# The experts of ranks 2 to 7 of a second mixture, written out twice in the arms of a conditional

## The chip, the cores and the metric

The kernel runs on one core of one Trainium2 chip. It is one launch that computes a local attention and two mixtures of experts. The metric is the device time of that launch in microseconds (us). TensorE (PE) does the matmuls, PEld loads their weights, VectorE (DVE), ScalarE (ACT) and GpSimd (POOL) do the rest; SyncE (SP) and other engines issue the transfers. Each engine runs its own instructions in order, and waits for others by semaphores.

## The reference

Attention over 4 x 8 x 576 x 64 gives 2304 tokens of 512 numbers. They go through a first mixture (a token has one expert, and some tokens skip it), and the result `x` goes through a second, in which each token has two of eight experts:

```python
def _moe2_ref(x, w_gate, w_noise, noise, w1, w2):     # x: 2304 x 512, w1: 8 x 512 x 1024, w2: 8 x 1024 x 512
    logits = x @ w_gate
    noise_scale = np.log1p(np.exp(x @ w_noise))
    noisy_logits = logits + noise_scale * noise
    top2 = np.argpartition(-noisy_logits, 2, axis=1)[:, :2]
    ...
    for e in range(E):
        for k in range(2):
            mask = top2[:, k] == e
            ...
            h = np.maximum(x[mask] @ w1[e], 0.0)
            out[mask] += top2_w[mask, k, None] * (h @ w2[e])
```

How many tokens an expert has depends on the data. Worked out from the reference with the inputs as it draws them (seed 0), experts 0 to 7 of the second mixture have 578, 590, 570, 587, 592, 562, 548 and 581 tokens.

## The kernel before

The attention runs first, then the first mixture, then the second. In the second mixture an expert is an object `Second` with a fixed capacity: a number of token rows that its matmuls work on, whatever its count is. Experts 0 and 1 are always first, with a capacity of 640 (five blocks of 128 rows, `NB2 = 5`, `BLK2 = 128`). The others are ranked by their counts on the chip, and the expert of rank r gets `CAPS2[r]` rows. Tokens beyond a capacity would go to a loop at the end (`over2`, in a conditional on `n_over2`).

The steps of an expert are these:

- `gather` (POOL, L317 within): five indirect transfers fetch the rows of its blocks (`rows2`, five buffers).
- `prep(b)`: four transposes on PE (`pT`, L1632) turn a block; ACT and DVE split it into a high and a low part (`xh`, `xl`, L1634 and L1635).
- `up(f)`, f from 0 to 7: matmuls on PE (`pH`, L1647), three products for each of four slices of the inner dimension, and for each chunk of tokens; then ACT writes `hh` (L1651) and DVE writes `hl` (L1652). For ranks 2 to 7 the tokens are in two chunks, 256 wide and `cap - 256` wide. For experts 0 and 1 they are in the chunks `first` (384 wide) and `second` (256 wide), and all eight `up(f, first)` come before the eight `up(f, second)`.
- `down(b)`: 24 matmuls 512 wide for each block (`pY`, L1664), ACT scales the result (`yo`, L1666), and POOL adds it to the output by an indirect transfer (L322).

The weights of an expert come in four pieces for each matrix through three buffers `stg` (SP), and ACT and DVE cut each piece into a high and a low part (L1322 and L1323).

While expert 1's `up(f, first)` runs, DVE ranks the experts and sets their places, and `gates` spreads the gate weights: three casts and two subtractions on DVE (L331 to L335), then two large multiplications on POOL (L346, `w<-w,g`, 128x2160). The orders of PE, ACT, DVE and SP are those in which the code is written; POOL's order is set by a scheduler, which moves no instruction across a conditional.

The first mixture has a conditional of the kind that the change adds (`small1`, L1829): `larger` takes four short DVE steps (L482, L484, L493, L213) to write `beyond`, the number of experts whose count is above the smaller capacities. `n_beyond` then reads that number into a register of each engine (TENSOR_LOAD, L1699), and each engine compares and jumps.

Of the kernel before, what the change touches and what calls it, by code (L numbers as in the profile page):

```python
# [21 lines left out]
DM = H * D  # L22
E = 8
# [11 lines left out]
BLK1, NB1 = 112, 2  # L35
CAPS = (224, 200, 180, 164, 152, 144, 132, 120)
CAPS_S, JOIN = (204, 178, 166, 150, 140, 136), 6
CAPS2 = (640, 640, 632, 616, 604, 596, 584, 572)
DUMP1 = E * NB1 * BLK1
BLK2, NB2 = 128, 5  # L40
# [67 lines left out]
def moe_attention_kernel(ctx, tc, q, k, v, w_skip, w_gate, w1, w2, g2, n2, noise, u1, u2, out, dbg=None):  # L108
# [58 lines left out]
    def routing_constants():  # L167
        c.desc = iota([128, E], [[-1, E]], E, 0, "desc")
        c.e64 = iota([128, E], [[64, E]], 0, 0, "e64")
        c.rows = iota([128, 128], [[1, 128]], 0, 0, "rows")  # L170
        c.codes1 = iota([128, E * NB1], [[64, E], [1, NB1]], 1, 0, "codes1")
        c.codes2 = iota([128, E * NB2], [[64, E], [1, NB2]], 1, 0, "codes2")
        c.dump1 = iota([128, E * NB1], [[BLK1, E * NB1]], N + 1, 1, "dump1")
        c.dump2 = iota([128, E * NB2], [[0, E], [BLK2, NB2]], N + 1, 1, "dump2")
        tkf = rt.tile([128, NT, 2], F32, name="tkf")
        nc.gpsimd.iota(tkf[:, :, 0], pattern=[[128, NT]], base=0, channel_multiplier=0,
                       allow_small_or_imprecise_dtypes=True)
        nc.gpsimd.iota(tkf[:, :, 1], pattern=[[0, NT]], base=1, channel_multiplier=1,
                       allow_small_or_imprecise_dtypes=True)
        c.tk = rt.tile([128, NT, 2], BF, name="tk")  # L180
        nc.gpsimd.tensor_copy(c.tk, tkf)
        c.number = iota([128, E], [[1, E]], 0, 0, "number")
        c.caps, c.caps_s, c.caps2, c.fixed = (rt.tile([128, E], F32, name=n) for n in ("caps", "capss", "caps2", "fixed"))
        nc.gpsimd.memset(c.fixed, 0.0)
        for r in range(E):
            nc.gpsimd.memset(c.caps[:, r:r + 1], float(CAPS[r]))
            nc.gpsimd.memset(c.caps_s[:, r:r + 1], float((CAPS_S + CAPS[JOIN:])[r]))
            nc.gpsimd.memset(c.caps2[:, r:r + 1], float(CAPS2[r]))
        for r in range(AHEAD):
            nc.gpsimd.memset(c.fixed[:, r:r + 1], float(AHEAD - r))  # L190
        c.steps = iota([128, 40], [[1, 40]], 0, 0, "steps")
        t = iota([128, E, E], [[1, E], [-1, E]], 0, 0, "upto")
        nc.gpsimd.tensor_scalar(t, t, 0.0, None, op0=OP.is_ge)
        c.upto = t
        c.dump2_ahead = iota([128, AHEAD * (CH[0][1] // BLK2)], [[0, AHEAD], [BLK2, CH[0][1] // BLK2]], N + 1, 1, "dump2a")
# [19 lines left out]
    class Places:  # L215
# [140 lines left out]
    def run(steps, n=1000):  # L356
        for f in steps[:n]:
            f()
        del steps[:n]
# [942 lines left out]
    slots1[2:2] = [weight_slot(F32) for i in range(2)]  # L1302
    split = {}

    def split_weights(name, e, r=None):

        src = (u1 if name == 1 else u2)
        src = (src[e:e + 1] if r is None else src[ds(r, 1)]).rearrange("o (k p) f -> p (o k) f", p=128)
        c = src.shape[2]
        st = {}  # L1310

        def load():
            split[name, e] = (weight_slot(F32R), weight_slot(F32R))
            k = 1024 // c
            for i in range(4):
                st[i] = stg.tile([128, 1024], F32, name="stg")
                nc.sync.dma_start(st[i].rearrange("p (k f) -> p k f", f=c), src[:, i * k:(i + 1) * k, :])

        def cut(i):
            hi, lo = split[name, e]  # L1320
            c = slice(i * 1024, (i + 1) * 1024)
            nc.scalar.activation(hi[:, c], st[i], AF.Copy)  # L1322
            V.tensor_tensor(lo[:, c], st[i], hi[:, c].bitcast(F32), op=OP.subtract)  # L1323

        return load, [lambda i=i: cut(i) for i in range(4)]
# [276 lines left out]

    adds, h2 = [], []

    class Second:


        def __init__(self, e):
            self.e, self.cap, self.rows, self.x = e, CAPS2[e], [], {}
            self.chunks = CH if e < AHEAD else ((0, 256), (256, self.cap))  # L1610

        def block(self, b):
# [1 line left out]

        def gather(self, n, idx):
            for b in range(n):
                r = xp.tile([BLK2, DM + 16], F32, name="rows2", bufs=5)
                s = self.block(len(self.rows))
                m = s.stop - s.start
                gather(r[0:m], idx[0:m, b:b + 1])  # L1620
                self.rows.append(r)

        def prep(self, b):
            cols = self.block(b)
            n = cols.stop - cols.start
            a, z = next(ch for ch in self.chunks if ch[0] <= cols.start < ch[1])
            if a == cols.start:
                w = 256 if z - a == 256 else 384
                self.x[a, z] = [xp.tile([128, KD, w], F32R, name=f"{name}{int(w == 256)}") for name in ("xh", "xl")]
            p = bank("pT", [128, KD, n])  # L1630
            for k in range(KD):
                nc.tensor.transpose(p[:, k, :], self.rows[b][0:n, k * 128:(k + 1) * 128], ident[0:n, 0:n])  # L1632
            hi, lo = (t[:, :, cols.start - a:cols.stop - a] for t in self.x[a, z])
            nc.scalar.activation(hi, p, AF.Copy)  # L1634
            V.tensor_tensor(lo, p, hi.bitcast(F32), op=OP.subtract)  # L1635

        def up(self, f, chunks=None):
            chunks = chunks or self.chunks
            if f == 0 and chunks[0][0] == 0:
                self.h = [h2[0].tile([128, KF, CAP], F32R, name=n) for n in ("hh", "hl")]  # L1640
            wh, wl = (t.rearrange("p (k f) -> p k f", k=KD) for t in split[1, self.e])
            ps = [bank("pH", [128, b - a]) for a, b in chunks]
            fs = slice(f * 128, (f + 1) * 128)
            for k in range(KD):
                for i, (w, n) in enumerate(((wh, 0), (wh, 1), (wl, 0))):
                    for p, ch in zip(ps, chunks):
                        nc.tensor.matmul(p, w[:, k, fs], self.x[ch][n][:, k, 0:ch[1] - ch[0]], start=k == 0 and i == 0,  # L1647
                                         stop=k == KD - 1 and i == 2)
            for p, (a, b) in zip(ps, chunks):
                hi, lo = (t[:, f, a:b] for t in self.h)  # L1650
                nc.scalar.activation(hi, p, AF.Relu)  # L1651
                V.scalar_tensor_tensor(lo, p, 0.0, hi.bitcast(F32), op0=OP.max, op1=OP.subtract)  # L1652
# [256 lines left out]
    for f in range(KF):  # L1909
# [7 lines left out]
        elif f > 2:  # L1917
# [2 lines left out]
                run(cb, 1)  # L1920
            elif f < 7:
                x.prep(f - 5 + EARLY)
    run(gates)
    gidx2, sidx2 = whole.gidx, whole.sidx
    for f in range(KF):
        x.up(f, second)
        if f % 2:
            run(cb, 1)
    whole.gate_table()
    over2 = Overflow(lambda: whole.total, BLK2, NB2 - 1, 34, Carved(rt.tile([128, NT * BLK1 // 2], F32, name="room2", tag="lhs1")), rt,  # L1930
                     "ov2", cap_of)
    for e in range(1, E):
        x = ex2[e]
        ca = cb = []
        if e + 1 < E:
            r = nc.sync.value_load(order2[0:1, e + 1:e + 2], min_val=0, max_val=E - 1)
            la, ca = split_weights(1, e + 1, r)
            lb, cb = split_weights(2, e + 1, r)
            ex2[e + 1].gather(NB2, gidx2[:, (e + 1) * NB2:(e + 2) * NB2])
            la()  # L1940
        if e > 1:
            for f in range(KF):
                x.up(f)
                if f % 2:
                    run(ca, 1)
                elif e == 3:
                    run(over2.steps, 4)
        if e + 1 < E:
            lb()
        for b in range(NB2):  # L1950
            if e + 1 < E:
                if b == 0:
                    ex2[e + 1].prep(0)
                    ex2[e + 1].prep(1)
                elif b < 4:
                    ex2[e + 1].prep(b + 1)
            i = e * NB2 + b
            x.down(b, gt2[:, i:i + 1], sidx2[:, i:i + 1])
            for w in range(2 if e == 1 else 1):
                run(ca or cb, 1)  # L1960
    n_over2, ids2 = over2.number(), over2.ids
    with tc.If(n_over2 > 0):
        with tc.For_i(0, n_over2, 1) as i:
# [90 lines left out]
```

## Time and profile before

| what | value |
|---|---|
| median of 3 runs | 773.49 us (771.2 to 775.84) |
| the profiled execution | 766.73 us, of which its span is 765.0 us, with 1.73 us around it |
| PE busy in the span | 743.2 us (97%) |
| DVE, ACT, POOL busy | 348.6 us, 249.2 us, 254.4 us |
| second mixture: its first matmul to the span's end | 298.3 to 765.0 us |
| expert 1's `up(f, first)` and `up(f, second)` on PE | 360.06 to 391.5 us |
| experts of ranks 2 to 7, `up(0)` of the first to PE's last `down` | 423.98 to 758.45 us |

A busy time is what an engine worked, and not what it was waited for; the chain of waits tells which engine's work ended last at each point. [...]

### The profile page before, as it was taken

How to read it: one execution, taken by the hardware profiler on the slowest of the kernel's cores; microseconds unless marked ns; L12 is line 12 of the kernel's file. 1: busy time of each engine (PE TensorE's matmuls, PEld its weight loads, DVE VectorE, ACT ScalarE, POOL GpSimd, SP SyncE). 2: the span in 40 equal slices, each digit the busy share in tenths (PEclk: the TensorE clock that was granted, in tenths of full speed). 3: DMA queues.
4: the chain of work that ended last, by engine and by line, in shares of the span. 5: the costliest groups of instructions: out<-in, count | busy, mean ns of one | idle time of the engine just before them, and what ended most of it. 6: DMA issues, size and time to landing. Idle time of an engine off the chain costs nothing.

```text
span 765.0 us, 15204 instructions
## 1 busy us (share of the span) xinstructions
PE 743.2 (97%) x6217; PEld 655.7 (86%) x6217; DVE 348.6 (46%) x789; ACT 249.2 (33%) x492; POOL 254.4 (33%) x272
## 2 busy tenths in 40 slices
PE   6989899999999999999999999999999999999996
PEld 3567777999999999888998998998997997987984
DVE  6986887411112755659654343343342342342200
ACT  3445653111112243233335333233332333333211
POOL 8783422321223541133545015015025124003012
PEclk9899999999999999999999999999999999999999
DMA  8999559699998952234538436336336337233013
GB/s 280 302 283 292 150 169 331 163 387 386 350 331 283 354 166 65 95 61 122 158 97 223 132 112 162 83 111 162 81 122 155 83 120 171 75 97 43 9 21 42
DMA packets 60396, 130.59 MB, mean 171 GB/s; under 512 B 15674, under 2 KB 16496, under 8 KB 58784
## 3 DMA queue, kind: packets, MB, share of 16 engines
q1 hardware_dynamic: 30688, 55.85, 23.4%
q10 hardware_dynamic: 17248, 46.66, 17.2%
q0 software_dynamic: 12384, 27.03, 16.7%
q8 instruction: 51, 0.84, 0.4%
q14 instruction: 25, 0.20, 0.1%
HBM read 101.86 MB, written 23.73 MB: 164 GB/s over the span
## 4 chain that ended last, share of the span: by engine, by line
PE 84%; DMA 5%; DVE 3%; POOL 3%; issue 3%; ACT 1%; ACTq 0%; DVEq 0%; POOLq 0%; SPq 0%
PE pY L1664 28%; PE pH L1647 25%; PE pH L584 9%; PE pY L599 9%; PE pT L1632 2%; DMA v<-in_v 1%; DMA kT<-in_k 1%; DMA x_d<-x 1%; PE pB L1019 1%; PE pT L621 1%; PE pT L1036 1%; PE pB L895 1%; PE pT L563 1%; DMA up<-od 1%; DMA rows<-x_d,ix2g 1%
## 5 line engine op out<-in xcount | busy, mean ns | idle before, releaser
L1664 PE MATMUL pY<-w,hh 128*128 128x512 f32 (+6 forms) x640 | 202.4, 397 | 0.0
L1647 PE MATMUL pH<-xh,w 128*128 128x256 f32 (+7 forms) x1024 | 195.3, 302 | 0.1
L1647 PEld LDWEIGHTS pH<-xh,w 128*128 128x128 f32 x1024 | 162.3, 188 | 1.0 <-DVE hl L1652 0.3
L1664 PEld LDWEIGHTS pY<-w,hh 128*128 128x128 f32 (+6 forms) x640 | 115.1, 183 | 28.3
L1323 DVE TENSOR_TENSOR w<-stg,w 128x1024 fp32r<-128x1024 f32 x64 | 83.0, 1303 | 108.5 <-ACT w L1322 108.3
L1664 PE MATMUL pY<-w,hl 128*128 128x512 f32 (+6 forms) x320 | 126.1, 394 | 0.0
L1647 PE MATMUL pH<-xl,w 128*128 128x256 f32 (+7 forms) x512 | 123.0, 301 | 0.0
L1652 DVE SCALAR_TENSOR_TENSOR hl<-pH,hh 128x256 fp32r<-128x256 f32 (+7 forms) x128 | 56.9, 473 | 127.9 <-ACT hh L1651 127.7
L322 POOL DMA_INDIRECT out<-yo,ix2w x35 | 67.7, 1934 | 131.0 <-ACT yo L1666 121.7
L1651 ACT ACTIVATE hh<-pH 128x256 fp32r<-128x256 f32 (+7 forms) x128 | 49.2, 423 | 150.8 <-PE pH L1647 150.7
L1647 PEld LDWEIGHTS pH<-xl,w 128*128 128x128 f32 x512 | 90.1, 188 | 0.0
L317 POOL DMA_INDIRECT rows<-x_d,ix2g x32 | 36.4, 1139 | 155.4 <-PE pT L1632 144.1
L1664 PEld LDWEIGHTS pY<-w,hl 128*128 128x128 f32 (+6 forms) x320 | 58.6, 183 | 15.7
L1322 ACT ACTIVATE w<-stg 128x1024 fp32r<-128x1024 f32 x64 | 67.0, 1055 | 8.1 <-DMA stg<-in_moe_w 8.1
L1666 ACT ACTIVATE yo<-pY,gt 128x512 f32<-128x512 f32 (+6 forms) x35 | 24.1, 687 | 138.9 <-PE pY L1664 78.0
L599 PE MATMUL pY<-hT,w 128*128 128x92 f32 (+7 forms) x512 | 65.3, 288 | 0.0
L599 PEld LDWEIGHTS pY<-hT,w 128*128 128x128 f32 x512 | 63.8, 190 | 0.2
L584 PE MATMUL pH<-xT,w 128*128 128x178 f32 (+6 forms) x448 | 62.6, 293 | 0.0
L584 PEld LDWEIGHTS pH<-xT,w 128*128 128x128 f32 x448 | 57.8, 190 | 1.6 <-issue 1.4
L322 POOL DMA_INDIRECT l_d<-x,ix1w x15 | 14.9, 995 | 84.2 <-DVE x L629 72.1
L602 DVE COPY yT<-pY 128x184 f32<-128x184 f32 (+7 forms) x16 | 7.2, 447 | 70.3 <-PE pY L599 70.3
L1030 POOL TENSOR_TENSOR x<-x,up 128x512 f32<-128x512 f32 x15 | 19.9, 1334 | 38.4 <-DMA up<-od 14.1
(425 smaller groups left out, 846.2 us busy)
## 6 DMA issues: line engine op xcount, KB each, us to landing
w<-in_moe_w ACTq DMA_DIRECT2D x16, 2048.0 KB, 13.0
stg<-in_moe_w SPq DMA_DIRECT2D x64, 512.0 KB, 3.9
x_d<-x SPq DMA_DIRECT2D x18, 264.0 KB, 6.0
out<-zero ACTq DMA_DIRECT2D x3, 1536.0 KB, 8.3
qT<-in_q SPq DMA_DIRECT2D x3, 1152.0 KB, 5.7
vw<-in_v SPq DMA_DIRECT2D x18, 192.0 KB, 5.7
vw<-in_v ACTq DMA_DIRECT2D x18, 192.0 KB, 6.2
v<-in_v SPq DMA_DIRECT2D x3, 1024.0 KB, 11.2
```

The lines of the kernel that those rows point to most:

```text
L317: return nc.gpsimd.indirect_dma_start(out=dst, out_offset=None, in_=x_d[0:n + 1], in_offset=bass.IndirectOffsetOnAxis(ap=idx, axis=0))
L322: return nc.gpsimd.indirect_dma_start(out=dst, out_offset=bass.IndirectOffsetOnAxis(ap=idx, axis=0), in_=src, in_offset=None, **kw)
L584: nc.tensor.matmul(self.p[:, j], w[:, k, f * 128:(f + 1) * 128], self.xT[:, k], start=k == 0, stop=k == KD - 1)
L599: nc.tensor.matmul(p[:, j], w[:, f, d * 128:(d + 1) * 128], self.hT[:, f], start=f == 0, stop=f == KF - 1)
L1030: e.tensor_tensor(xs[t][:, 0:DM], xs[t][:, 0:DM], ups[t], op=OP.add)
L1322: nc.scalar.activation(hi[:, c], st[i], AF.Copy)
L1323: V.tensor_tensor(lo[:, c], st[i], hi[:, c].bitcast(F32), op=OP.subtract)
L1647: nc.tensor.matmul(p, w[:, k, fs], self.x[ch][n][:, k, 0:ch[1] - ch[0]], start=k == 0 and i == 0, stop=k == KD - 1 and i == 2)
L1651: nc.scalar.activation(hi, p, AF.Relu)
L1652: V.scalar_tensor_tensor(lo, p, 0.0, hi.bitcast(F32), op0=OP.max, op1=OP.subtract)
L1664: nc.tensor.matmul(p, h[:, f], w[:, f], start=f == 0 and i == 0, stop=f == KF - 1 and i == 2)
L1666: nc.scalar.activation(o, p, AF.Copy, scale=gate[0:n])
```

## The change

Ranks 2 to 7 of the second mixture are now written out twice, by a function `experts2(caps)`. One arm of a conditional `small2` has the capacities `CAPS2_S` and is taken if no expert's count is above them, the other has the old `CAPS2`. For ranks 2 to 7 the capacities are 616, 604, 596, 576, 576, 564 instead of 632, 616, 604, 596, 584, 572: 72 rows fewer in all. Since both arms must use the same buffers, the tiles for rows, for `xh`/`xl`, for `hh`/`hl` and the three pairs for weights are taken ahead of the conditional (`homes2`, `pairs`), in the rotation that they had. The counts of the reference's inputs lie below `CAPS2_S`, by 6 tokens at the least (rank 5: 570 of 576).

```diff
+CAPS2_S = (640, 640, 616, 604, 596, 576, 576, 564)
 CAPS2 = (640, 640, 632, 616, 604, 596, 584, 572)
...
             nc.gpsimd.memset(c.caps2[:, r:r + 1], float(CAPS2[r]))
+            nc.gpsimd.memset(c.caps2_s[:, r:r + 1], float(CAPS2_S[r]))
...
-    run(gates)
+    run(gates + larger(lambda: whole.total, c.caps2_s))
+    n_beyond = nc.values_load(beyond[0:1, 0:1], min_val=0, max_val=E,
+                              skip_runtime_bounds_check_because="a count of experts")
     gidx2, sidx2 = whole.gidx, whole.sidx
     for f in range(KF):
+        if f == KF - 3:
+            tc.mark_branch_hint_location("small2", "LikelyTaken", [E_.PE, E_.Activation, E_.DVE])
         x.up(f, second)
         if f % 2:
             run(cb, 1)
     whole.gate_table()
     over2 = Overflow(lambda: whole.total, BLK2, NB2 - 1, 34, Carved(rt.tile([128, NT * BLK1 // 2], F32, name="room2", tag="lhs1")), rt,
                      "ov2", cap_of)
-    for e in range(1, E):
-        x = ex2[e]
...
+    class homes2:
+        rows = [xp.tile([BLK2, DM + 16], F32, name="rows2", bufs=5) for b in range(NB2)]
+        x = {w: x_tiles(w) for w in (256, 384)}
+        h = ex2[1].h
+
+    pairs = [(weight_slot(F32R), weight_slot(F32R)), split[1, 1], split[2, 1]]
+    def experts2(caps):
+        ex2[2:] = [Second(e, caps[e], homes2) for e in range(2, E)]
+        over_steps = list(over2.steps)
+        for e in range(1, E):
...
+                r = nc.sync.value_load(order2[0:1, e + 1:e + 2], min_val=0, max_val=E - 1)
+                la, ca = split_weights(1, e + 1, r, pairs[2 * (e - 1) % 3])
+                lb, cb = split_weights(2, e + 1, r, pairs[(2 * e - 1) % 3])
+                ex2[e + 1].gather(NB2, gidx2[:, (e + 1) * NB2:(e + 2) * NB2])
+                la()
...
+    with tc.If(n_beyond <= 0, label="small2", preferred_fallthrough_block=False) as small2:
+        experts2(CAPS2_S)
+    with small2.Else():
+        experts2(CAPS2)
```

What is left out of `experts2` is the old loop's body. In the lists of instructions the change moves or adds rows at three places. Lines of the kernel after are 3 to 7 higher than those of before.

On PE, where expert 1's chunk `first` (384 wide) ends and `second` (256 wide) begins. Before:

```order
L1647 MATMUL pH<-xh_5337,w 128x384 x2
L1647 MATMUL pH<-xl_5338,w 128x384
L1647 MATMUL pH<-xh_5337,w 128x384
L1647 MATMUL pH<-xh_5725,w 128x256
L1647 MATMUL pH<-xl_5726,w 128x256
```

After:

```order
L1653 MATMUL pH<-xh_5346,w 128x384 x2
L1653 MATMUL pH<-xl_5347,w 128x384
L1653 MATMUL pH<-xh_5346,w 128x384
L1930 TENSOR_LOAD beyond
L1653 MATMUL pH<-xh_5734,w 128x256
L1653 MATMUL pH<-xl_5735,w 128x256
```

The load of `beyond` into PE's register now stands between the last matmul of `up(7, first)` and the first of `up(0, second)`; the jump itself comes later, after `gate_table`.

On DVE, at the same place: the low halves `hl` of expert 1, and after the last of `first` the new steps. Before:

```order
L1635 TENSOR_TENSOR xl_5726<-pT,xh_5725 128x4x128
L1652 SCALAR_TENSOR_TENSOR hl<-pH,hh 128x384
L1652 SCALAR_TENSOR_TENSOR hl<-pH,hh 128x256 x2
L1323 TENSOR_TENSOR w_5520<-stg,w_5519 128x1024
L1652 SCALAR_TENSOR_TENSOR hl<-pH,hh 128x256 x2
```

After:

```order
L1658 SCALAR_TENSOR_TENSOR hl<-pH,hh 128x384
L485 TENSOR_TENSOR above<-rank_of,caps2s 128x64
L487 TENSOR_REDUCE smallof<-above 128x8
L496 TENSOR_TENSOR smallof<-total_4945,smallof 128x8
L216 TENSOR_REDUCE beyond<-smallof 1x1
L1930 TENSOR_LOAD beyond
L1658 SCALAR_TENSOR_TENSOR hl<-pH,hh 128x256 x2
```

The four steps that write `beyond` stand behind the last `hl` of `up(7, first)`, which waits for PE's last matmul of that chunk.

On POOL, around the two multiplications of `gates` (`rows_5666` and `rows_5668` are the last blocks of expert 1, the DMA rows after them the blocks of the expert of rank 2). Before:

```order
L317 DMA rows_5666<-x_d,ix2g 128x528
L317 DMA rows_5668<-x_d,ix2g 128x528
L317 DMA rows_5949<-x_d,ix2g 128x528
L317 DMA rows_5951<-x_d,ix2g 128x528
L317 DMA rows_5953<-x_d,ix2g 128x528
L317 DMA rows_5955<-x_d,ix2g 128x528
L346 TENSOR_TENSOR w<-w,g_4935 128x2160 x2
L317 DMA rows_5957<-x_d,ix2g 120x528
```

After:

```order
L320 DMA rows_5675<-x_d,ix2g 128x528
L320 DMA rows_5677<-x_d,ix2g 128x528
L349 TENSOR_TENSOR w<-w,g_4944 128x2160 x2
L1930 TENSOR_LOAD beyond
L1981 COMPARE_AND_BRANCH
L320 DMA rows_5963<-x_d,ix2g 128x528
L320 DMA rows_5964<-x_d,ix2g 128x528
L320 DMA rows_5965<-x_d,ix2g 128x528
```

Four gathers of rank 2 that stood ahead of the multiplications now stand behind them, behind POOL's load of `beyond` and its jump.

## Rows read from the trace of the kernel before

**Rows 1.** Busy us of PE, PEld, DVE, ACT, POOL, granted clock, ranks 2 to 7.

```profile
395.00:750.00 355.00, 355.00 (x2068) 315.73 (x2067) 120.43 (x190) 116.56 (x206) 91.48 (x58) 1.00 0.43 108
```

**Rows 2.** Chain that ended last, ranks 2 to 7 (start us, us, what).

```profile
412.32 0.41 PE pT L1632 x4
412.73 11.24 PE pY L1664 x48
423.98 27.52 PE pH L1647 x192
...
638.53 0.25 PE pT L1632 x4
...
705.46 24.96 PE pH L1647 x192
```

**Rows 3.** Timeline of PE in expert 1's up (start us, us, what).

```profile
379.96 0.28 PE L1647 MATMUL pH<-xl,w 128*128 128x256 f32 x1
```

**Rows 4.** Timeline of ACT there.

```profile
380.04 0.49 ACT L1651 ACTIVATE hh<-pH 128x384 fp32r<-128x384 f32 x1 [1.50 <-PE pH L1647]
```

**Rows 5.** Timeline of DVE there.

```profile
375.31 0.19 DVE L335 CAST g<-w 128x36 bf16<-128x36 f32 x1
...
380.56 0.56 DVE L1652 SCALAR_TENSOR_TENSOR hl<-pH,hh 128x384 fp32r<-128x384 f32 x1 [1.30 <-ACT hh L1651]
...
384.23 3.94 DVE L1323 TENSOR_TENSOR w<-stg,w 128x1024 fp32r<-128x1024 f32 x1 [0.52 <-ACT w L1322]
```

**Rows 6.** Timeline of POOL there.

```profile
372.14 1.52 POOL L317 DMA_INDIRECT rows<-x_d,ix2g  x1 [0.30 <-issue]
...
379.51 7.57 POOL L346 TENSOR_TENSOR w<-w,g 128x2160 bf16<-128x2160 bf16 x2
```

**Rows 7.** Timeline of DVE at the first mixture's conditional.

```profile
137.95 0.26 DVE L482 TENSOR_TENSOR above<-rank_of,capss 128x64 f32<-128x64 f32 x1
...
138.76 0.15 DVE L213 TENSOR_REDUCE beyond<-smallof 1x1 int32<-1x8 f32 x1
```

**Rows 8.** Line L1699, PE's load of the register (count, ns, start us).

```profile
L1699 PEldq TENSOR_LOAD <-beyond x1: 491/491/491, 142.8 to 142.8; - x1
```

**Rows 9.** Timeline of PE at that conditional's jump.

```profile
142.94 1.95 PE L599 MATMUL pY<-wide,w 128*128 128x112 f32 x16
144.72 0.48 PE L584 MATMUL pH<-xTb,w 128*128 128x92 f32 x3
```

**Rows 10.** Timeline of DVE behind that jump.

```profile
142.20 0.17 DVE L1745 TENSOR_SCALAR key<-rank 128x8 f32<-128x8 f32 x1 [1.07 <-issue]
```

**Rows 11.** Timeline of POOL, earlier multiplications of the same line.

```profile
342.16 2.60 POOL L346 TENSOR_TENSOR w<-w,tk 128x1440 bf16<-128x1440 bf16 x1 [5.14 <-issue]
```

**Rows 12.** Timeline of DVE beside and behind it.

```profile
343.30 3.87 DVE L342 TENSOR_TENSOR w<-rows,row 128x2304 bf16<-128x2304 f32 x1
...
358.08 2.55 DVE L342 TENSOR_TENSOR w<-rows,row 128x2304 bf16<-128x2304 f32 x1
```

**Rows 13.** DVE's line L1323, all 64 (ns min/median/max).

```profile
L1323 DVE TENSOR_TENSOR w<-stg,w x64: 1207/1225/3943, 269.9 to 701.7; 128x1024 fp32r<-128x1024 f32 x64
```

**Rows 14.** Busy time by stretch early in the kernel (PEclk is the granted clock).

```profile
7.87:10.59 2.72, 0.01 (x1) 0.03 (x1) 1.46 (x5) 0.23 (x1) 2.72 (x2) 1.00 0.85 280
...
12.00:15.40 3.40, 3.40 (x55) 2.04 (x44) 1.83 (x5) 0.97 (x2) 2.91 (x15) 0.50 0.96 303
...
19.33:25.20 5.87, 5.03 (x46) 2.12 (x48) 5.66 (x12) 3.04 (x7) 5.39 (x44) 0.50 0.99 313
...
41.50:43.50 2.00, 0.01 (x1) 0.00 (x0) 0.93 (x3) 0.12 (x1) 1.92 (x3) 1.00 1.06 297
```

**Rows 15.** Timeline of PE in expert 1's second chunk.

```profile
388.20 0.75 PE L1647 MATMUL pH<-xh,w 128*128 128x256 f32 x2
```

**Rows 16.** Transfers by line on the page (count, KB, us from issue to landing).

```profile
stg<-in_moe_w SPq DMA_DIRECT2D x64, 512.0 KB, 3.9
```

**Rows 17.** Timeline of POOL behind its early memsets.

```profile
28.92 1.28 POOL L788 TENSOR_TENSOR kd<-kT 128x576 f32<-128x576 f32 x1 [4.03 <-DMA kT<-in_k]
```

More of the change, by code (lines that the diff above doesn't have):

```diff
@@ L182, in routing_constants @@
         c.number = iota([128, E], [[1, E]], 0, 0, "number")
-        c.caps, c.caps_s, c.caps2, c.fixed = (rt.tile([128, E], F32, name=n) for n in ("caps", "capss", "caps2", "fixed"))
+        c.caps, c.caps_s, c.caps2, c.caps2_s, c.fixed = (rt.tile([128, E], F32, name=n)
+                                                         for n in ("caps", "capss", "caps2", "caps2s", "fixed"))
         nc.gpsimd.memset(c.fixed, 0.0)
@@ L1303, in moe_attention_kernel, with split_weights @@
     split = {}
-    def split_weights(name, e, r=None):
+    def split_weights(name, e, r=None, homes=None):
         src = (u1 if name == 1 else u2)
@@ L1312, in load @@
         def load():
-            split[name, e] = (weight_slot(F32R), weight_slot(F32R))
+            split[name, e] = homes or (weight_slot(F32R), weight_slot(F32R))
             k = 1024 // c
@@ L1603, in moe_attention_kernel, with x_tiles, __init__ @@
     adds, h2 = [], []
+    def x_tiles(w):
+        return [xp.tile([128, KD, w], F32R, name=f"{name}{int(w == 256)}") for name in ("xh", "xl")]
     class Second:
-        def __init__(self, e):
-            self.e, self.cap, self.rows, self.x = e, CAPS2[e], [], {}
+        def __init__(self, e, cap=None, homes=None):
+            self.e, self.cap, self.rows, self.x, self.homes = e, cap or CAPS2[e], [], {}, homes
             self.chunks = CH if e < AHEAD else ((0, 256), (256, self.cap))
@@ L1616, in gather @@
             for b in range(n):
-                r = xp.tile([BLK2, DM + 16], F32, name="rows2", bufs=5)
+                r = self.homes.rows[b] if self.homes else xp.tile([BLK2, DM + 16], F32, name="rows2", bufs=5)
                 s = self.block(len(self.rows))
@@ L1628, in prep @@
                 w = 256 if z - a == 256 else 384
-                self.x[a, z] = [xp.tile([128, KD, w], F32R, name=f"{name}{int(w == 256)}") for name in ("xh", "xl")]
+                self.x[a, z] = self.homes.x[w] if self.homes else x_tiles(w)
             p = bank("pT", [128, KD, n])
@@ L1639, in up @@
             if f == 0 and chunks[0][0] == 0:
-                self.h = [h2[0].tile([128, KF, CAP], F32R, name=n) for n in ("hh", "hl")]
+                self.h = self.homes.h if self.homes else [h2[0].tile([128, KF, CAP], F32R, name=n) for n in ("hh", "hl")]
             wh, wl = (t.rearrange("p (k f) -> p k f", k=KD) for t in split[1, self.e])
@@ L1931, in moe_attention_kernel @@
                      "ov2", cap_of)
-    for e in range(1, E):
-        x = ex2[e]
[L1934 to L1950, printed above, removed]
-            if e + 1 < E:
[L1952 to L1960, printed above, removed]
+    class homes2:
+        rows = [xp.tile([BLK2, DM + 16], F32, name="rows2", bufs=5) for b in range(NB2)]
+        x = {w: x_tiles(w) for w in (256, 384)}
+        h = ex2[1].h
@@ new lines, in moe_attention_kernel @@
+    pairs = [(weight_slot(F32R), weight_slot(F32R)), split[1, 1], split[2, 1]]
[3 more added lines that the diff above has]
+        for e in range(1, E):
+            x = ex2[e]
+            ca = cb = []
+            if e + 1 < E:
+                r = nc.sync.value_load(order2[0:1, e + 1:e + 2], min_val=0, max_val=E - 1)
[3 more added lines that the diff above has]
+                la()
+            if e > 1:
+                for f in range(KF):
+                    x.up(f)
+                    if f % 2:
+                        run(ca, 1)
+                    elif e == 3:
+                        run(over_steps, 4)
+            if e + 1 < E:
+                lb()
+            for b in range(NB2):
+                if e + 1 < E:
+                    if b == 0:
+                        ex2[e + 1].prep(0)
+                        ex2[e + 1].prep(1)
+                    elif b < 4:
+                        ex2[e + 1].prep(b + 1)
+                i = e * NB2 + b
+                x.down(b, gt2[:, i:i + 1], sidx2[:, i:i + 1])
+                for w in range(2 if e == 1 else 1):
+                    run(ca or cb, 1)
```

## The prediction

> **What bounds the kernel now.** I read the busy time by stretch first. Through the experts of ranks 2 to 7 PE is busy for all of 355 us, at a granted clock of 1.00, while DVE, ACT and POOL each work about a third of the time or less [rows 1]. The chain that ended last then shows how: `up`, `down` and transposes of PE follow one another without a gap [rows 2]. So this stretch costs what PE's instructions take. A shorter matmul shortens the kernel by as much, and a halt of PE lengthens it by as much, for nothing behind it has slack that could take it up. The change does both, so I cost PE's work that goes, and then every wait that comes.
>
> **What goes.** `up` of one expert is 192 matmuls, 96 of them as wide as the second chunk. With a capacity of 632 they take 27.52 us, with 572 they take 24.96 us [rows 2], which is 2.56 us for 60 rows or 0.0427 us for each row. 72 rows fewer give 3.07 us. The transposes of the last block take 0.41 us at 120 rows and 0.25 us at 72 [rows 2], 0.0033 us for each row, so 72 give 0.24 us. `down` gives nothing: its matmuls stay 512 wide and 24 to a block, 48 in 11.24 us [rows 2], and the rows only fill the weights' side. Smaller pieces for ACT, DVE and the transfers lie beside PE. The sum is 3.31 us.
>
> **The load of `beyond` on PE.** This is the part that costs. The load stands between `up(7, first)` and `up(0, second)` of expert 1, and waits until DVE has written `beyond`. DVE can do that only behind the last `hl` of the same `up(7, first)`, so the wait runs from PE through ACT and DVE and back to PE, and all matmuls of `second` queue behind it. PE would start `second` at 379.96 [rows 3]. ACT's `hh` runs from 380.04 for 0.49 us [rows 4], and DVE's `hl` ends at 380.56 + 0.56 = 381.12 [rows 5]. The four new steps are those of the first conditional, which took from 137.95 to 138.76 + 0.15, that is 0.96 us [rows 7]: `beyond` is there at 382.1. PE's load takes 0.49 us [rows 8], so PE goes on at 382.6. That is 2.6 us of halt if nothing else holds DVE.
>
> POOL does hold it, I think. Before, POOL's two multiplications ran from 379.51 for 7.57 us, behind four gathers of the next expert [rows 6]. Now only expert 1's two gathers are ahead of them; these end at 372.14 + 1.52 = 373.7 [rows 6], and the last cast that they wait for ends at 375.5 [rows 5]. They then run from 375.5 to 383.1. The first new step of DVE multiplies two tiles of SBUF and is due at 381.1, in the middle of the second one. What such a meeting does is in the trace twice. DVE's L1323, also with two operands in SBUF, took 3.94 us from 384.23 [rows 5] where its median is 1.225 us [rows 13]: it ended one full length after POOL did (379.51 + 7.57 = 387.08). L342 took 3.87 us from 343.30 where the same line took 2.55 us at 358.08 [rows 12], and POOL's earlier multiplication ended at 342.16 + 2.60 = 344.76 [rows 11], again one full length ahead of DVE's end. An `hl`, which reads one operand from PSUM, went through beside POOL in its 0.56 us [rows 5].
>
> [...]
>
> So the first step starts at 383.1, `beyond` is there at 384.05, and PE goes on at 384.05 + 0.49 = 384.55. The halt is 4.6 us. I take this end, since the two rows are the same pair of engines with the same kinds of operands; 2.6 us is the other bound. No lower bound is a gain, for the load cannot begin ahead of `beyond`.
>
> **What follows from the halt.** PE stood still for 2.72 us from 7.87, and the granted clock was 0.50 from 12.00 to 15.40, while PE was busy again; after an idle stretch of 2.00 us at 41.50 it had stayed at 1.00 in that stretch [rows 14]. [...] The bounds are 0 and, from the stretch of 5.87 us at 0.50 [rows 14], 2.9 us.
>
> One loss of before goes. Two matmuls at 388.20 took 0.75 us [rows 15] instead of about 0.40, since DVE was held in the L1323 just named until 388.1 [rows 5]. POOL's multiplications are now over at 383.1, so this 0.35 us is saved.
>
> **What I cost at nothing.** *The jump.* At the first conditional PE's matmuls ran from 142.94 for 1.95 us, and the first one behind the jump started at 144.72 [rows 9]: no gap, for matmuls already queued covered the load, the comparison and the jump. At the new jump the matmuls of `gate_table` are the cover. If that is too thin, the upper end is 1.07 us, DVE's whole idle time for its load and jump together [rows 10]. *The gathers.* Rank 2's gathers start behind POOL's load and jump, at about 385 instead of 374. PE was still in `second` at 388.20 [rows 15], and is later by the halt now; two gathers of 1.5 us each [rows 6] are out by 388 and land before PE's transposes, which come behind `second` and `gate_table`. With that cover gone each gather would cost its 1.5 us. *SP's loads* wait for buffers that DVE frees in `second`, and shift with PE. *Eight more memsets* on POOL stand ahead of a wait of 4.03 us for a transfer [rows 17]. *The fixed tiles* have the rotation of before.
>
> **The sum.** -3.31 - 0.35 + 4.6 + 1.7 = +2.6 us. The profiled execution had a span of 765.0 us and a time of 766.73 us, so 769.4 us there; it lay 6.8 us under the median of the runs shown, against which I state the forecast: 773.5 + 2.6 = **776.1 us**, 0.34% above. A difference under 0.5% (3.9 us) is about what a measurement of this kernel cannot tell from no change.
>
> **The rivals.**
>
> *POOL doesn't hold DVE.* The small step slips between the two multiplications, or POOL is late. The halt is then 2.6 us and the sum +0.6 us: **774.1 us**. For it: the new step is far shorter than the lines that were seen held. Against it: both of those waited for POOL's end, whatever their own length.
>
> *The wait hides.* PE has work queued as the load waits, or `beyond` comes in time; then only the gain is left, **770.2 us**. For it: at the first conditional PE never halted [rows 9]. Against it: there the load stood behind matmuls that did not feed `beyond`; here it waits for the very last of them.
>
> *The code of the arm is not at hand.* The jump goes over the whole other arm, nearly 2,000 matmuls of PE with their weight loads in the list of instructions. If what lies behind must be fetched then, PE waits for a transfer; the nearest row is 3.9 us from issue to landing [rows 16]. The time is 776.1 + 3.9 = **780.0 us**, slower by 0.8%; it decides from about 1.3 us of halt at the jump on. Against it: no gap at the first jump, whose hint stands at the head of its block as this one's does. [...] No row of before shows such a wait.
>
> *The large arm is run.* The change then saves nothing: 776.1 + 3.3 = **779.4 us**. For it: ranks 5 and 6 have 6 and 14 tokens to spare at seed 0, and other inputs can exceed them. Against it: the reference's own inputs do not.
>
> **How the numbers follow.** The forecast has 0.54, POOL not holding DVE 0.18, the hidden wait 0.07, the fetch 0.15, the large arm 0.06. The forecast's own range is 774.4 (no lower clock) to 778.4 us (2.9 us of clock and 1.07 us at the jump). The range goes from 772.4 us, the second case without the lower clock, to 780.0 us, the fetch; it leaves out the hidden wait and about half of the two slow cases. Slower by over 0.5% (above 777.4 us) are the fetch, the large arm and the upper fifth of the forecast: 0.32. Faster by over 0.5% is half of the hidden wait, 0.04. The rest, 0.64, is within 0.5%.
>
> **What would show it.** In the profile after: `up` of ranks 2 to 7 from 27.0 down to 24.6 us; one idle time of PE of 4 to 5 us ahead of `up(0, second)` of expert 1, put down to DVE's `beyond`; POOL's two multiplications from about 375.5; DVE's first new step (L485) 2 us late and ending with POOL's; a granted clock of 0.50 for some 3.4 us behind the halt; no gap at the jump. The forecast is wrong if PE's idle time there is under 2 us, if the clock stays at 1.00, or if there is a second gap behind `gate_table`.

## The result, and the profile after

The kernel after takes 777.6 us (median of 20 runs, 773.3 to 780.0), the kernel before, run beside it, 773.0 us (20 runs, 769.3 to 779.8). The ratio is **1.0052, interval 1.0034 to 1.0071**: slower by about 4.0 us by the ratio (the two medians are 4.6 us apart), where 776.1 us (+2.6) was forecast. At 0.52% it lies just past the 0.5% that the forecast gave 0.32 to be passed.

The profiled execution of after has a span of 776.9 us. That is 11.9 us more than before's 765.0, three times the 4.0 us of the ratio, so most of it can't be the change. The chain of waits says where to cut. In it `up(0, first)` of expert 1 starts at 368.57 us, and at 360.22 us in the profile of before: 8.3 us are there before the first wait that the change moves. I therefore compare the *rest* of an execution, from that start to the end of the span: 404.8 us before, 408.3 after. A second profile of before and one with only the new memsets, both below, have rests of 405.4 and 405.2 us. Against the mean of these three, 405.1 us, after's rest is longer by 3.2 us. (Only two kernels were profiled twice, before and the one with the sizes alone below; their rests repeat within 0.6 and 0.2 us.)

The chain that ended last in after, around the halt (start us, us, what):

```profile
368.57 2.10 PE pH L1653 x12
...
386.79 2.11 PE pH L1653 x12
...
388.92 0.50 ACT hh L1657
...
389.44 0.56 DVE hl L1658
390.00 1.55 DVE above L485
...
392.10 0.16 DVE beyond L216
392.26 0.57 issue
392.82 13.08 PE pH L1653 x96
405.90 1.91 PE pT L354 x36
407.81 1.05 PE pT L1638 x8
408.86 5.57 PE pY L1670 x24
...
438.04 27.02 PE pH L1653 x192
```

The chain leaves PE after `first`, goes through ACT's `hh`, DVE's `hl` and the new steps, and comes back to PE. Behind it the jump leaves no mark on PE: `gate_table` (L354), the transposes and `down` follow on each other.

The timeline of after at that place, all engines (start us, us, engine, line, operation, and in brackets the idle time ahead and what ended it):

```profile
383.89 7.56 POOL L349 TENSOR_TENSOR w<-w,g 128x2160 bf16<-128x2160 bf16 x2 [1.90 <-DVE g L338]
...
389.92 1.62 DVE L485 TENSOR_TENSOR above<-rank_of,caps2s 128x64 f32<-128x64 f32 x1
...
392.82 0.36 PE L1653 MATMUL pH<-xh,w 128*128 128x256 f32 x1 [3.94 <-DVE beyond L216]
...
396.05 0.98 POOL L320 DMA_INDIRECT rows<-x_d,ix2g  x1 [4.60 <-DVE hl L1658]
```

DVE's L485 takes 1.62 us, where the same step took 0.26 us at the first conditional [rows 7]. It ends at 391.54, 0.09 us behind POOL's multiplications at 383.89 + 7.56 = 391.45.

The busy time by stretch in after (us of PE, PEld, DVE, ACT, POOL, granted clock, transfers), as [rows 14] for before. The granted clock is the share of TensorE's full clock that the profile gives for a stretch.

```profile
388.88:392.80 3.92, 0.00 (x1) 0.01 (x1) 2.63 (x5) 0.49 (x1) 2.57 (x1) 1.00 0.00 0
392.80:394.00 1.20, 1.18 (x10) 1.20 (x11) 0.00 (x0) 0.00 (x0) 0.00 (x0) 1.00 0.06 20
394.00:397.40 3.40, 3.40 (x19) 3.40 (x18) 0.42 (x1) 0.50 (x2) 1.04 (x2) 0.51 0.12 23
397.40:406.00 8.60, 8.60 (x77) 8.55 (x76) 4.82 (x8) 4.03 (x9) 3.79 (x4) 0.99 0.89 311
```

PE stands still for 3.94 us, then works 1.2 us at 1.00, then 3.4 us at 0.51. The 96 matmuls of `second` take 13.08 us.

PE's load of `beyond` in after, by line L1930 (count, ns min/median/max, start us):

```profile
L1930 PEldq TENSOR_LOAD <-beyond x1: 328/328/328, 392.3 to 392.3; - x1
```

The jump's instructions on POOL and PE in after, by line L1981:

```profile
L1981 POOLq COMPARE_BRANCH  x1: 58/58/58, 393.0 to 393.0; - x1
...
L1981 PEldq COMPARE_BRANCH  x1: 350/350/350, 406.7 to 406.7; - x1
```

The gain, on the chain of after, as [rows 2]:

```profile
494.75 26.57 PE pH L1653 x192
551.04 26.24 PE pH L1653 x192
607.37 25.44 PE pH L1653 x192
662.64 25.39 PE pH L1653 x192
717.88 24.64 PE pH L1653 x192
```

With the 27.02 us above, the six `up` add up to 155.30 us; in the chain of before they add up to 157.48. That is a gain of 2.18 us. What counts for the time is the whole way from the end of `second` to the end of the span. In before `second` ends with this piece of the chain:

```profile
388.56 3.10 PE pH L1647 x24
```

From 391.66 to 765.0 that way is 373.3 us in before, and from 392.82 + 13.08 = 405.90 to 776.9 it is 371.0 in after: the gain of the smaller sizes is 2.3 us. (Before's second profile and the one with only the memsets have 373.3 and 373.4.) So the change costs 3.94 us of halt and 1.7 to 1.8 us of clock and gives 2.3, which is +3.4 us; the rest shows +3.2.

### The profile page after: what moved, and what is told of

Read it like the earlier page. It is cut to its first block, busy times and chain, and to the rows that moved or that the text cites. A ratio compares the mean times of both kernels' runs of the same rounds, so it can differ in the third digit from the quotient of the medians.

```text
span 776.9 us, 15321 instructions
## 1 busy us (share of the span) xinstructions
PE 743.7 (96%) x6216; PEld 655.3 (84%) x6217; DVE 348.3 (45%) x793; ACT 247.9 (32%) x492; POOL 250.4 (32%) x280
## 4 chain that ended last, share of the span: by engine, by line
PE 82%; DMA 7%; DVE 3%; POOL 3%; issue 2%; ACT 2%; another core or an unknown queue 1%; ACTq 0%; DVEq 0%; SPq 0%; POOLq 0%
PE pY L1670 27%; PE pH L1653 26%; PE pH L587 9%; PE pY L602 8%; PE pT L1638 2%; DMA x_d<-x 2%; DMA v<-in_v 1%; DMA kT<-in_k 1%; PE pB L1022 1%; PE pT L566 1%; PE pT L624 1%; PE pT L1039 1%; DMA stg<-in_moe_w 1%; PE pT L354 1%
## 5 line engine op out<-in xcount | busy, mean ns | idle before, releaser
L1670 PE MATMUL pY<-w,hh 128*128 128x512 f32 (+5 forms) x640 | 201.9, 397 | 0.0
L1653 PE MATMUL pH<-xh,w 128*128 128x256 f32 (+6 forms) x1024 | 195.3, 302 | 3.9 <-DVE beyond L216 3.9
L1670 PEld LDWEIGHTS pY<-w,hh 128*128 128x128 f32 (+5 forms) x640 | 114.1, 182 | 29.1
L1326 DVE TENSOR_TENSOR w<-stg,w 128x1024 fp32r<-128x1024 f32 x64 | 80.3, 1261 | 112.4 <-ACT w L1325 111.7
L1670 PE MATMUL pY<-w,hl 128*128 128x512 f32 (+5 forms) x320 | 125.8, 393 | 0.0
L1653 PE MATMUL pH<-xl,w 128*128 128x256 f32 (+6 forms) x512 | 123.0, 301 | 0.0
L1658 DVE SCALAR_TENSOR_TENSOR hl<-pH,hh 128x256 fp32r<-128x256 f32 (+6 forms) x128 | 56.2, 469 | 128.9 <-ACT hh L1657 128.2
L1657 ACT ACTIVATE hh<-pH 128x256 fp32r<-128x256 f32 (+6 forms) x128 | 48.7, 420 | 152.6 <-PE pH L1653 152.6
L1670 PEld LDWEIGHTS pY<-w,hl 128*128 128x128 f32 (+5 forms) x320 | 58.1, 182 | 15.8
L1672 ACT ACTIVATE yo<-pY,gt 128x512 f32<-128x512 f32 (+5 forms) x35 | 24.1, 687 | 136.4 <-PE pY L1670 75.6
L590 ACT ACTIVATE hT<-pH 128x184 f32<-128x184 f32 (+7 forms) x32 | 12.7, 401 | 62.3 <-PE pH L587 43.8
```

The source lines that it names most:

```text
L1670: nc.tensor.matmul(p, h[:, f], w[:, f], start=f == 0 and i == 0, stop=f == KF - 1 and i == 2)
L1672: nc.scalar.activation(o, p, AF.Copy, scale=gate[0:n])
```

## The experiments

My theory: the change loses by the halt (3.94 us) and the lower clock behind it, and POOL's multiplication makes the halt longer than it need be. The rivals: the two arms cost by themselves (the jump, code, later gathers); the change costs something in the first 360 us. Each ratio is to the kernel before on the same chip. The rests come from one profile each. A *hint* is the call `mark_branch_hint_location` ahead of a jump, with the jump's label, `LikelyTaken` and a list of engines; the change lists PE, ACT and DVE and not POOL. What it does on the chip is read from the runs alone.

**The load of `beyond` later.**

```diff
     run(gates + larger(lambda: whole.total, c.caps2_s))
-    n_beyond = nc.values_load(beyond[0:1, 0:1], ...)
     for f in range(KF):
         if f == KF - 3:
+            n_beyond = nc.values_load(beyond[0:1, 0:1], ...)
             tc.mark_branch_hint_location("small2", ...)
```

> The load of `beyond` into the registers is moved from ahead of `up(0, second)` of expert 1 to ahead of `up(5, second)`; everything else is as after. My theory is that the load costs the halt (3.94 us), its own 0.33 us and the lower clock behind the halt (about 1.9 us), 6.2 us in all. Then PE has no idle time over 0.5 us in `second`, the clock stays at 1.00, and the time is after's 777.6 - 6.2 = 771.4 us, a ratio to before of 0.998 (0.996 to 0.9995). Rival A, the two arms themselves cost (the jump, code, POOL's later gathers): the halt goes and as much comes back behind `gate_table`, ratio 1.003 to 1.005. Rival B, the loss lies ahead of the new load, where the profiled execution of after was some 8 us later than that of before already: the halt goes, but expert 1's `up(f, first)` starts at about 368 us once more instead of 360, ratio at least 1.002.

Measured: ratio 1.0012 (0.9986 to 1.0037), rest 404.9 us. The halt is gone and the clock stays at 1.00 in `second` (385.9 to 397.0 us), but only 3.4 of the expected 6.2 us come back in the rest, and the ratio misses the expected 0.996 to 0.9995. New idle times stand behind `gate_table`. The timeline of this kernel, with the first gather of rank 2 on POOL and the two first transposes on PE:

```profile
393.30 1.78 POOL L320 DMA_INDIRECT rows<-x_d,ix2g  x1 [4.59 <-PE pH L1653]
...
401.01 0.63 PE L1638 MATMUL pT<-ident,rows 128*128 128x128 f32 x4 [1.84 <-DMA rows<-x_d,ix2g]
402.02 0.63 PE L1638 MATMUL pT<-ident,rows 128*128 128x128 f32 x4 [0.38 <-DMA rows<-x_d,ix2g]
```

The chain of the same kernel goes from PE's wait back to POOL's jump:

```profile
389.36 0.15 DVE beyond L216
...
390.26 0.06 POOLq L1981
390.32 2.24 issue
```

Behind its jump POOL issues nothing for 2.24 us, with no wait that the trace names. My theory fell short here: the halt in after had been the cover of the gathers, and with the halt gone they are late by 1.84 + 0.38 = 2.2 us.

**POOL gets the hint too.** The kernel just shown, with POOL in the hint's list.

```diff
-            tc.mark_branch_hint_location("small2", "LikelyTaken", [E_.PE, E_.Activation, E_.DVE])
+            tc.mark_branch_hint_location("small2", "LikelyTaken", [E_.PE, E_.Activation, E_.DVE, E_.Pool])
```

> The kernel with the later load, and the hint on the coming jump given to POOL too, not only to PE, ACT and DVE. In the kernel with the later load POOL jumps at 390.3 us and its next gather starts at 393.30, with 2.24 us in which it waits for nothing that the trace shows, and PE waits 2.2 us for rows that come too late. My theory: POOL waits there for the code behind its jump. Then with the hint those 2.2 us go, the first gather starts within 1 us of the jump, PE's waits for rows behind `gate_table` fall from 2.2 us to under 0.5, and the time is that of the kernel with the count earlier, ratio 0.998. Rival, the 2.2 us are the software's making of a gather or the wait for the buffers: the gap stays, ratio 1.001.

Measured: ratio **0.9975 (0.9954 to 0.9996)**, rest 402.7 us, 2.2 less than without it. POOL's jump in this kernel, by line L1981:

```profile
L1981 POOLq COMPARE_BRANCH  x1: 78/78/78, 384.7 to 384.7; - x1
```

And its next gather, in POOL's timeline:

```profile
385.95 1.30 POOL L320 DMA_INDIRECT rows<-x_d,ix2g  x1 [2.46 <-PE pH L1653]
```

From jump to gather it takes 1.25 us instead of 3.0, and PE's wait for the rows is gone: behind `gate_table` the chain goes over PE alone. So 1.75 us of POOL's wait go with the hint. What POOL waited for the trace does not name; that it was the code behind the jump was my guess, and is not shown. The gather came 1.25 us behind the jump and not within the 1 us that I expected; what is gained suffices.

**The count earlier.** The four steps run ahead of `up(0, first)`; load and hint are those of after.

```diff
-    run(half1)
+    run(half1 + larger(lambda: whole.total, c.caps2_s))
...
-    run(gates + larger(lambda: whole.total, c.caps2_s))
+    run(gates)
```

> The four DVE steps that write `beyond` are moved ahead of `up(0, first)` of expert 1, behind the ranking; the load stays where after has it. My theory: PE's load finds `beyond` written for 20 us and takes its 0.33 us without a halt, the clock stays at 1.00, POOL's multiplications hold nothing on the path; time as with the later load, 771 to 772 us, ratio 0.998 (0.996 to 0.9995). Rival A, two arms cost by themselves: ratio 1.003 to 1.005. Rival C, it is the load's place and not the wait for the four steps (PE must run empty for a load that stands between matmuls): an idle time of 1 us or more is left ahead of `up(0, second)`, ratio about 1.000 to 1.002.

Measured: ratio 0.9981 (0.9958 to 1.0005), rest 402.8 us. The load stands where it stood and costs nothing; in the chain `second` begins without a gap (108 matmuls are the last 12 of `first` and the 96 of `second`):

```profile
383.70 13.39 PE pH L1653 x108
397.09 1.91 PE pT L354 x36
399.00 1.05 PE pT L1638 x8
```

The rest is 5.5 us less than after's. Of this 3.94 are the halt; the clock is 13.08 - (13.39 - 2.11) = 1.80 us, by after's row of 12 at 2.11. POOL's jump is issued early here, at 381.6 us, so that a wait behind it fits beside its multiplications (they end at 388.51, and the next gather starts at 388.66). It is the wait for the steps that costs, not the place of the load.

**No hint at all.** The count earlier, without the hint.

```diff
     for f in range(KF):
-        if f == KF - 3:
-            tc.mark_branch_hint_location("small2", "LikelyTaken", [E_.PE, E_.Activation, E_.DVE])
         x.up(f, second)
```

> The count earlier, with the hint on the coming jump taken from PE, ACT and DVE too. It tests my prediction's rival that the arm's code is not at hand. If it is the hint that has the code ready, PE now waits behind its jump as POOL did (2.24 us): PE's gap behind `gate_table` is 1 to 4 us, the ratio 1.000 to 1.003. If the code is at hand anyway, there is no gap, and the ratio is 0.998 as with the hint.

Measured: ratio 1.0006 (0.9981 to 1.0031), rest 407.6 us, 4.8 more than with the hint (0.6 of it ahead of the jump, in `first`). The jump on PE in this kernel, by its line:

```profile
L1979 PEldq COMPARE_BRANCH  x1: 3675/3675/3675, 400.6 to 400.6; - x1
```

PE's timeline behind it:

```profile
404.44 1.94 PE L1638 MATMUL pT<-ident,rows 128*128 128x128 f32 x8 [2.76 <-issue]
```

And the busy time by stretch:

```profile
401.68:404.44 2.76, 0.00 (x1) 0.03 (x1) 1.49 (x3) 0.00 (x0) 0.00 (x0) 0.92 0.04 12
404.44:405.60 1.16, 1.16 (x6) 1.16 (x7) 0.00 (x0) 0.00 (x0) 0.00 (x0) 0.50 0.06 14
405.60:409.00 3.40, 3.40 (x14) 2.86 (x13) 1.38 (x2) 1.20 (x2) 1.93 (x2) 0.74 0.36 94
```

The compare and jump takes 3675 ns instead of the 350 of the kernel with the hint, PE stands still for 2.76 us, and the granted clock falls to 0.50 in the 1.16 us behind that. A wait behind the jump, as the prediction's rival had it, is a real cost here, and on PE the hint takes it away. What PE waits for the trace does not say. The profile's rest lies 2.5 us above the 405.1 of before, the ratio says only +0.5 us, with an interval up to +2.4. Against the best conditional, below and on the same chip, the ratios are 0.0045 apart, which is 3.5 us.

**POOL's multiplications later.** The last cast that POOL waits for is issued behind the four steps.

```diff
-            run(gates, 2)
+            run(gates, min(2, len(gates) - 3))
...
-    run(gates + larger(lambda: whole.total, c.caps2_s))
+    run(larger(lambda: whole.total, c.caps2_s) + gates)
```

> As after, but POOL's two multiplications come behind the steps that write `beyond`: the last cast that POOL waits for is issued behind the four steps. My theory (POOL's multiplication holds DVE's first step): that step takes 0.26 us instead of 1.6 to 1.9, `beyond` is there about 1.4 us earlier and PE's halt is 2.5 to 2.7 us instead of 3.94; the multiplications (7.6 us) then run from about 391 to 399 us, hold DVE's splitting of weights (L1326) in `second` once more, and the gathers of rank 2 start only behind them. Time: after less 1.4 us, given back in part by the later gathers, ratio 1.003 to 1.006. Rival, the first step is slow by itself or waits for something else than POOL: it stays at 1.6 us or more and the halt at 3.9 us.

Measured: ratio 1.0037 (1.0021 to 1.0054), rest 408.2 us. The timeline of this kernel:

```profile
387.87 0.25 DVE L485 TENSOR_TENSOR above<-rank_of,caps2s 128x64 f32<-128x64 f32 x1
...
389.03 7.57 POOL L349 TENSOR_TENSOR w<-w,g 128x2160 bf16<-128x2160 bf16 x2 [9.38 <-DVE g L338]
...
389.45 0.36 PE L1653 MATMUL pH<-xh,w 128*128 128x256 f32 x1 [2.62 <-DVE g L338]
...
395.45 2.24 DVE L1326 TENSOR_TENSOR w<-stg,w 128x1024 fp32r<-128x1024 f32 x1 [0.52 <-ACT w L1325]
...
405.70 0.63 PE L1638 MATMUL pT<-ident,rows 128*128 128x128 f32 x4 [0.82 <-DMA rows<-x_d,ix2g]
```

With POOL out of the way the step takes 0.25 us and the halt 2.62 us, 1.32 less. That is the short end that the prediction had named. Now POOL (389.03 + 7.57 = 396.60) holds L1326, which ends 1.09 us behind it at 397.69; and rank 2's gathers, behind the multiplications, make PE wait 0.82 us. So only 0.5 us are won behind `first`, and `first` itself took 0.3 us longer in this execution, which leaves 0.1 us in the rest. The clock falls all the same. The busy time of the stretch behind the halt:

```profile
391.00:394.40 3.40, 3.40 (x21) 3.40 (x20) 0.42 (x1) 0.70 (x3) 3.40 (x2) 0.60 0.21 58
```

**The halt filled.**

```diff
     run(gates + larger(lambda: whole.total, c.caps2_s))
+    p = bank("pY", [128, 512])
+    for i in range(16):
+        nc.tensor.matmul(p, warm[:, 0:128], warm, start=True, stop=True)
     n_beyond = nc.values_load(...)
```

> As after, with 16 matmuls 512 wide on a constant tile ahead of PE's load of `beyond`, whose result nothing reads: about 3.4 us of work in the time in which PE stands still otherwise. My theory: the wait for `beyond` ends as late as in after (about 3.9 us behind the last matmul of `first`), but since PE worked in it the granted clock stays at 1.00 behind it, and the 96 matmuls of `second` take 11.2 to 11.5 us instead of 13.1: about 1.7 us less than after, ratio 1.003. The rival that `second` is slower for another reason than the clock (banks, DVE or ACT late): it stays at 13 us, ratio 1.005.

Measured: ratio 1.0026 (1.0008 to 1.0044), rest 407.0 us. PE's timeline here:

```profile
382.80 3.63 PE L1932 MATMUL pY<-warm 128*128 128x512 bf16 x16
387.27 0.36 PE L1653 MATMUL pH<-xh,w 128*128 128x256 f32 x1 [0.84 <-DVE beyond L216]
```

And the stretch of `second`:

```profile
387.27:398.66 11.39, 11.39 (x97) 11.35 (x97) 5.25 (x9) 4.58 (x9) 5.70 (x5) 1.00 0.55 176
```

The wait ends 4.30 us behind `first`, 0.4 later than in after, since DVE's first step is held for longer here (1.99 us). But the clock stays at 1.00 and `second` takes 11.55 us in the chain: 1.5 us come back there by work that computes nothing, and 1.3 in the rest. So the loss behind the halt is the clock.

**The old sizes in both arms**: the cost alone.

```diff
     with tc.If(n_beyond <= 0, label="small2", preferred_fallthrough_block=False) as small2:
-        experts2(CAPS2_S)
+        experts2(CAPS2)
```

> Both arms have the old capacities, so that the conditional is there and nothing is gained by it. My theory: the halt and the clock as after (3.5 to 4.5 us of halt, about 1.9 us of clock), `up` of ranks 2 to 7 back at 157.5 us in sum, so after's time and 2.2 to 3.3 us more: 780 to 781 us, ratio 1.008 to 1.0095. The rival that the smaller sizes save nothing here: ratio as after, 1.005.

Measured: ratio 1.0095 (1.0058 to 1.0132), rest 410.7 us, 2.4 more than after. The halt is 4.18 us, and the six `up` are back at 157.68 us.

**The sizes alone**, in the kernel before, with no conditional.

```diff
-CAPS2 = (640, 640, 632, 616, 604, 596, 584, 572)
+CAPS2 = (640, 640, 616, 604, 596, 576, 576, 564)
```

On inputs with larger counts the loop at the end would take the excess.

> The kernel before with the smaller capacities in place of the old ones and no conditional. With the reference's inputs no expert exceeds them, so the output is the same. My theory: the gain alone, `up` of ranks 2 to 7 shorter by 2.2 (the rows of after) to 3.1 us (72 rows at 0.0427 us) and the transposes by up to 0.24 us: 769.7 to 770.8 us, ratio 0.9957 to 0.997; no halt in expert 1. The rival that the smaller sizes save nothing: ratio 1.000.

Measured: ratio **0.9949 (0.9927 to 0.9972)**, rest 402.5 us, 2.6 under the 405.1 of before; the ratio lies below the expected 0.9957 to 0.997, which its interval reaches. The six `up` add up to 154.60 us. In the chain `second` ends with this piece:

```profile
381.09 13.40 PE pH L1647 x108
```

From 394.49 to the end of the span at 765.5 it is 371.0 us, as in after.

**The early part.** The kernel before once more, and the kernel before with the new tile and its memsets alone:

```diff
...
             nc.gpsimd.memset(c.caps2[:, r:r + 1], float(CAPS2[r]))
+            nc.gpsimd.memset(c.caps2_s[:, r:r + 1], float((640, 640, 616, 604, 596, 576, 576, 564)[r]))
```

> The kernel before once more, for a second profile. In the five kernels profiled besides it, expert 1's `up(f, first)` starts between 363.0 and 368.6 us, in the profile of before at 360.2. If that start varies by the execution (the landing of the first loads), it lies later than 361 us here; if the change moves it, at about 360 us again.

> The kernel before with one more small tile and its eight memsets on POOL at the start, all that the change does ahead of expert 1. My theory: they stand ahead of POOL's wait for the first transfers and cost nothing: ratio 1.000 (0.9985 to 1.0015). The rival that this moves the first 300 us: 1.002 or more.

Measured: in before's second profile expert 1's `up(f, first)` starts at 358.1 us, which by itself is on the side of the rival; the rest is 405.4 us. With the memsets the ratio is 0.9984 (0.9956 to 1.0012). There the start is at 369.4 us, the latest of all fourteen profiles, though the kernel has no conditional; and in the kernel with POOL's hint, which has all that the change does there, it is at 360.6. So the start varies by 11 us between profiles and does not follow the change (the same kernel profiled twice differs by about 2). On one chip, 34 of 35 runs of before alone lie between 768.1 and 779.4 us. The change's work there costs nothing that these runs can tell.

**The best conditional beside the sizes alone.** The first is the count earlier with the hint for POOL too.

> The count earlier and the hint for POOL together: nothing of the conditional is left on the path by my theory. Expert 1's `up(f, first)` to the end takes 402.5 to 403 us, as in the kernel with the sizes alone, no idle time of PE over 0.7 us there, ratio 0.997 (0.995 to 0.9985). Rival, a price of the conditional ahead of that point: ratio 0.998 to 1.000 while the sizes alone, on the same chip, are at 0.995.

> The sizes alone once more, to stand beside the best conditional on one chip. My theory: ratio 0.9965 (0.995 to 0.998), the same as the best conditional within the intervals. The rival that the conditional has a price early in the program: 0.995 or less, and at least 0.002 under the best conditional.

Measured on one chip: the count earlier with POOL's hint **0.9961 (0.9930 to 0.9991)**, rest 402.4 us; the sizes alone 0.9959 (0.9929 to 0.9990), rest 402.7 us. These runs cannot tell them apart: a conditional whose count is early and whose hint lists all four computing engines costs nothing here that can be measured (the intervals are 0.003, or 2.4 us, to either side).

## Why the prediction was right

The sum was +2.6 us, the rest shows +3.2 and the ratio +4.0 (2.6 to 5.5 by the interval). The mechanism held; the sizes of three terms did not, and that the sum came this near is in part luck. The gain was put 1.0 us too large and a saving of 0.35 us did not come, but the halt was put 0.66 us too long, which made up for half of that.

- *What bounds it*: right. PE's chain is unbroken on both sides of the halt, and what PE loses or gains there, the rest shows.
- *The gain*: too large, 3.31 us forecast and 2.3 measured. 72 rows at 0.0427 us were to give 3.07 us in `up`; the six `up` give 2.18 in after, and 2.88 in the kernel with the sizes alone, with the same widths. The 576-row experts take 25.44 and 25.39 us in after, 25.28 and 24.97 there; in `down` of the same chains after is faster by about as much, so that the whole way behind `second` is 371.0 us in both. The times repeat in both profiles of before and in both of the sizes alone. Why they move between `up` and `down` from program to program is open. The transposes were to give 0.24 us and give nothing: the last block's take 0.39 us at 64 rows, more than the 0.25 at 72 rows from which the prediction drew its line. In the chain of after, and in that of before for the 60 rows of its last expert:

```profile
595.77 0.39 PE pT L1638 x4
...
693.81 0.39 PE pT L1632 x4
```

- *The halt*: right in its cause, 3.94 us instead of 4.6. POOL did hold DVE's first step, which takes 0.25 us without POOL and 1.62 beside it; with POOL later the halt falls to 2.62 us, the prediction's other bound of 2.6. The step was held for 1.4 us and not 2.0, as POOL had less left to do (391.45 - 390.00): `first` ended 20.3 us behind its start, and 19.8 in the profile of before. The step ended 0.09 us behind POOL, and not its full length as the prediction had it. The load itself took 0.33 us, not 0.49.
- *The clock*: right, though no run had shown that a halt of 4.6 us brings 0.50: it was my estimate. The 1.7 us of the sum, between the bounds of 0 and 2.9, are half of the 3.40 us at 0.50 in [rows 14]. After shows 3.40 us at 0.51 behind 3.94 us of halt, and `second` takes 1.80 us more than without the halt, and 1.53 more than with the halt filled.
- *The 0.35 us saved*: not shown. The two L1326 in `second` take 1.23 and 1.22 us in after, so DVE is no longer held there. But only the first profile of before lost anything on PE in `second`: there L1323 took 3.94 us and `second` 11.7. In before's second profile `second` takes 11.3 us, as in the kernel with the count earlier:

```profile
376.82 13.41 PE pH L1647 x108
```

- *The jump*: nothing on PE, as said, but only by the hint. Without it PE loses 2.76 us and the clock behind it (0.50 for 1.16 us). That rival's 3.9 us were of the right size (3.5 us by the ratios on one chip, 4.8 by the rests), and the loss did not come because the hint lists PE. That PE waits for code there is not shown.
- *The gathers*: right in after, for a reason that the prediction had only in part. POOL's jump came when it was forecast, 24.4 us behind `up(0, first)` (393.0 - 368.57; 385 in the profile of before is 24.8). The first gather came 3.0 us after that, at 396.05; POOL is not in the hint's list, and in the kernel with the load later its place there made this 1.25 us instead of 3.0. The halt and the clock gave the cover. When the halt is taken away, 2.2 us of PE's time go to them.
- *The rivals*: that POOL does not hold DVE and that the wait hides are refuted by the halt of 3.94 us. That the large arm runs is refuted by the second chunk of the last expert, which is 564 - 256 = 308 wide in after (24.64 us for its `up`, 24.96 before):

```profile
L1653 PE MATMUL pH<-xh,w 128*128 128x308 f32 x64 | 17.9, 301 | 0.0
```

## What to carry to other kernels

Before a branch is added to an engine that never waits, follow the branched-on value back: if its last input comes behind that engine's newest work, the load is a round trip from that engine through the others and back, 3.94 us here, and a fall of the clock came on top that cost 1.80 us. Compute the value a stage earlier (5.5 us less in the rest here), and give the hint on the jump to each engine that has work behind it (on PE the jump took 350 ns with it and 3675 without), also to the one that only issues transfers there (behind POOL's jump the gather came 1.75 us sooner). When a halt is removed, look again at all that was "hidden": here the gathers had lived on the cover that it gave, and cost PE 2.2 us without it.

## What the runs showed of the hardware

- With the count earlier and no hint, PE's jump took 3675 ns and PE stood still for 2.76 us; with the hint it took 350 ns and there was no gap. With the load later, POOL issued nothing for 2.24 us behind its jump, and its gather came 3.0 us behind it; with POOL in the hint's list the gather came after 1.25 us.
- A halt of PE of 2.62 us was followed by a granted clock of 0.60 between 391.0 and 394.4 us in the kernel with POOL later, and one of 3.94 us in after by 0.51 between 394.0 and 397.4; with 16 matmuls on a constant tile in the halt, and 0.84 us of idle time left, it was 1.00 in `second`.
- DVE's 128x64 step on two SBUF tiles took 0.25 us by itself. In each of the four profiles whose rows show it beside POOL's 128x2160 multiplications it ended 0.08 to 0.09 us behind them: it took 1.62 us in after, 1.81 with the load later, 1.60 with POOL's hint and 1.99 with the halt filled. With the old sizes it took 1.86 us.
